# An attention and expert kernel on one Trainium2 core: the leftover keys' value product in four 64x64 tiles, and the order of the passes around it

## The chip, the cores and the metric

The kernel runs on one core of one Trainium2 chip. Its engines are named as the profile names them: PE (TensorE: matrix products, and transposes as products with the identity), DVE (VectorE), ACT (ScalarE), POOL (GpSimd) and SP (the queue that issues most DMAs). PE reads SBUF and writes PSUM, which has 8 banks of 2 KB in each of 128 partitions; DVE and ACT read PSUM and write SBUF.

The metric is the device time of one execution in microseconds (us). The kernel before was run three times: 1012.91, 1013.5 and 1015.62 us, a median of 1013.5.

## What is computed

Two stages. Eight batches of attention with 8 heads, 576 positions and head size 64, in which all probabilities below a threshold near the row's maximum are dropped; then its output, as 4608 rows of 512, goes through a router that gives each of 8 experts its 576 best rows, and through the experts.

```python
def _attn_ref(q, k, v, tau):
    scale = 1.0 / np.sqrt(q.shape[-1])
    scores = scale * np.matmul(q, k.transpose(0, 1, 3, 2))
    thresh = np.max(scores, axis=-1, keepdims=True) - tau
    scores = np.where(scores >= thresh, scores, -1000000000.0)
    scores = scores - np.max(scores, axis=-1, keepdims=True)
    attn = np.exp(scores)
    attn = attn / (np.sum(attn, axis=-1, keepdims=True) + 1e-09)
    return np.matmul(attn, v)
...
    for e in range(E):
        mask = assigned == e
        h = np.maximum(x[mask] @ w1[e], 0.0)
        out[mask] = h @ w2[e]
```

All products are in float32 in attention; the experts' use pairs of a rounded and a remainder part.

## The kernel before, in words

**Pairs, tiles, slots.** Attention takes two heads of a batch at a time: a pair `p`, four pairs a batch, 32 in all. A pair's scores are made in 9 tiles of 128 query rows by 576 keys (`score`, L70): tiles 0 to 7 alternate between the two heads, four each, and tile 8 holds the last 64 queries of both heads. Each tile `sc` has two PSUM banks, and the 576 keys stand as 288 columns in each; its two products use the two row halves of PE at once (64 rows by 128 columns), and tile 8 uses four tiles of 64x64 at once. A slot is two score tiles. The loop runs over 144 slots `s_`, and every engine works through its instructions in the order in which the loop emits them; each waits for what the others must have done first.

**What happens to a tile.** DVE scales it and takes its minimum (`mx`, L75, `z<-sc`), ACT takes the exponential (`ex`, L86), a slot later DVE drops what is below the threshold and sums (`stt`, L90), and one slot on PE transposes 512 of the 576 keys into the tile `tb` (`tr`, L99), two score tiles to one `tb`, of which there is one buffer of two banks. In the slot after that ACT copies them out to `pt` (`trev`, L114, L116).

**The leftover keys.** 64 keys of each row are left over: keys 512 to 575 of the first head and 0 to 63 of the second. Their transposes (`left`) go into the free columns behind the 288 of both `sc` buffers of one slot, the left slot: three of them into the first, two into the second. ACT copies them to `pl` (`leftev`, L125 to L127): the first head's keys to partitions 0 to 63, the second head's to 64 to 127. DVE's two passes `mx` of that slot are emitted behind all of these copies.

**The value product.** It is made transposed, in two halves `f` of 288 queries. A unit (`pv_unit`, L144) is two products of 128 keys by 64 columns, one for each head, side by side in the two column halves of one bank `xo`. Four units make one half, and `pl_unit` (L149) adds the leftovers to it, again as two products over all 128 partitions, with a `vt` that is zero where the other head's keys stand. So a pair has 8 units and 2 leftover units. When a half is done, ACT copies it to `xt` (L151).

**What sets the order.** A queue holds the units in order; at each slot's end `columns` takes from it as long as a credit lasts, which grows by 2.4 a slot up to 3.3, and as the unit's input is there (`when`). The first four units wait for tile 5's transposes, the others for tile 8's, the leftovers for `pl`. `xo` has two buffers, taken in turn by the halves and by `whole`, which fits in the batch's head work when no half is open: the sums' reciprocals (`rd_unit`, L165), the router's logits (`lg_unit`, L176, twice), their transposes (`lgt_unit`, L183, `lgm_unit`, L193) and, in the first two batches, five transposes of output rows (`xt_unit`, L205); those of the other batches come after the loop. `pt` has two buffers: before the first tile of pair p+2 is copied to it, the products of pair p must be done, and where they aren't, they are emitted in front of this copy (the `while` in the loop).

The diff touches `pv_unit`, `pl_unit`, `leftev`, `push_pair`, `columns`, `whole` and the loop.

Of the kernel before, what the change touches and what calls it, by code (L numbers as in the profile page):

```python
# [9 lines left out]
F32 = mybir.dt.float32  # L10
# [3 lines left out]
AF = mybir.ActivationFunctionType  # L14
# [8 lines left out]
def attention(ctx, tc, qk, vl, tau, wgd, xrows, xts, Lg, nb_batches, ident, swap, R, after_first):  # L23
    nc=tc.nc
# [6 lines left out]
    ps_t=ctx.enter_context(tc.tile_pool(name="ps_t",bufs=1,space=PSUM))  # L31
    ps_v=ctx.enter_context(tc.tile_pool(name="ps_v",bufs=2,space=PSUM))
    taub=cst.tile([128,1],F32,name="taub")
# [3 lines left out]
    LD={}  # L37
# [47 lines left out]
    def ex(t):  # L85
        A.activation(pview(t),ZB[t].rearrange("p a b -> p (a b)"),AF.Exp,bias=NBI[t][:,0:1],scale=-1.0)  # L86
# [8 lines left out]

    PT={}; PL={}; TB={}
    def turn(o,x):
# [12 lines left out]
    def trev(t):  # L110
        p,i=divmod(t,9); tb=TB.pop(t)
        if i==0: PT[p]=wk.tile([128,2,4,S],F32,name="pt"); PL[p]=wk.tile([128,S],F32,name="pl")
        if i<8:
            A.activation(PT[p][:,i%2,:,(i//2)*128:(i//2+1)*128].rearrange("p k (r q) -> p r k q",r=2),tb,AF.Copy)  # L114
        else:
            A.activation(PT[p][:,:,:,512:576],tb,AF.Copy)  # L116
    LB={}
    def left(p,n,t):
# [3 lines left out]
        if n: turn(sc[:,:,HS+64:HS+128],PB[p*9+8][:,512:640])  # L122
    def leftev(p):
        a=LB.pop((p,0)); b=LB.pop((p,1))
        A.activation(PL[p][:,0:384].rearrange("p (g r q) -> p r g q",g=3,r=2),a[:,:,HS:HS+192].rearrange("p r (g q) -> p r g q",g=3),AF.Copy)  # L125
        A.activation(PL[p][:,384:512].rearrange("p (r q) -> p r q",r=2),b[:,:,HS:HS+64],AF.Copy)
        for r in range(2): A.activation(PL[p][64*r:64*r+64,512:576],b[64*r:64*r+64,r,HS+64:HS+128],AF.Copy)  # L127

# [3 lines left out]

    banks=[]; VB={}
    def bank_v(sh):
        t=ps_v.tile(sh,F32,name="xo"); banks.append([False]); VB[id(t)]=banks[-1]
        return t
    def free_v(): return len(banks)<2 or banks[-2][0]
    def pv_unit(p,f,u):
        b,j=divmod(p,4)
        if b not in XT: XT[b]=wk.tile([128,4,S],F32,name="xt",bufs=XTB)  # L140
        if u==0: XO[p,f]=bank_v([128,512])
        xo=XO[p,f]; q=slice(f*HS,(f+1)*HS); v=LD[p]["v"]
        for h in range(2):
            T.matmul(xo[64*h:64*h+64,:HS],v[:,u,64*h:64*h+64],PT[p][:,h,u,q],start=(u==0),stop=False,skip_group_check=True)  # L144
    def pl_unit(p,f):
        b,j=divmod(p,4)
        q=slice(f*HS,(f+1)*HS); xo=XO.pop((p,f))
        for h in range(2):
            T.matmul(xo[64*h:64*h+64,:HS],LD[p]["v"][:,4,64*h:64*h+64],PL[p][:,q],start=False,stop=True,skip_group_check=True)  # L149
        if f==1: have[p,"pv"]=1  # L150
        return VB[id(xo)],lambda: A.activation(XT[b][:,j,q],xo[:,:HS],AF.Copy)  # L151
    def bank_g(b,sh):
        if b<nb_batches-1: return bank_v(sh)
# [47 lines left out]
    def xt_unit(b,c):  # L201
        ps=bank_v([128,4,128])
        n=128 if c<4 else 64
# [20 lines left out]
    def push_pair(p):  # L224
        b,j=divmod(p,4)
        def when(n): return lambda: have.get((p,n),1<<30)+HOLD<=st["slot"]
        if p==NP-1:


            def left(f):  # L230
                k,g=pl_unit(p,f); g(); k[0]=True
            for f in range(2):
                for u in range(4): queue.append(("c",when("t5" if f==0 else "t8"),u==0,lambda f=f,u=u: pv_unit(p,f,u)))
                if f==0: queue.append(("n",when("t8"),False,lambda: rd_calc(b)))
            for g in (lambda: rd_unit(b)(),lambda: left(0),lambda: left(1),lambda: lg_unit(b,0)(),lambda: lg_unit(b,1)(),lambda: lgt_unit(b)(),lambda: lgm_unit(b)()):
                queue.append(("n",when("pl"),False,g))
            queue.append(("n",lambda: not later,False,lambda: late.extend([lambda c=c: xt_unit(b,c) for c in range(5)])))
            return
        for f in range(2):
            for u in range(4): queue.append(("c",when("t5" if f==0 else "t8"),u==0,lambda f=f,u=u: pv_unit(p,f,u)))  # L240
            if (f,j)==(0,3): queue.append(("n",when("t8"),False,lambda: rd_calc(b)))
            queue.append(("c",when("pl"),False,lambda f=f: pl_unit(p,f)))
        if (b,j)==(0,0): queue.append(("n",lambda: True,False,R.consts))
        if (b,j)==(nb_batches-1,2): queue.append(("n",lambda: not aux,False,lambda: (R.prep(0,28),R.compare(R.k("E1"),J,0,28))))
        if j==3: queue.append(("n",lambda: not later,False,lambda: finish(b)))
    def finish(b):
# [6 lines left out]
    def flush():  # L253
        for k,g in later: g(); k[0]=True
        later.clear()
    def columns():
        while queue and queue[0][1]():
            if queue[0][0]=="c":
                if st["credit"]<1 or (queue[0][2] and not free_v()): return
                st["credit"]-=1  # L260
            c,_,_,g=queue.pop(0); r=g()
            if c=="c" and r:
                later.append(r)
                if aux: return
# [10 lines left out]
    after_first()  # L275
    ps=ps_v.tile([128,512],F32,name="xo")
# [93 lines left out]
class Router:  # L370
# [193 lines left out]
    def close(s): s.close1(); s.close2()  # L564
# [383 lines left out]
```

## Time and profile before

| What | us |
|---|---|
| median of three runs | 1013.5 |
| profiled execution, run time | 1010.9 |
| its span, first to last instruction | 1009.1 |
| attention's slots, about | 15 to 475 |
| router and experts | behind that |

The granted TensorE clock was 1.0 all through attention. A timeline row has the start in us from the span's start, the length in us from the first to the last of the merged instructions, engine, line, operation, out<-in, tile shape (for PE rows by columns of the array), operand shape and count; in square brackets the idle time before it and what ended it. A float32 product shows as two instructions, so that a value unit is x4 and a score tile is x4 (x8 where tile 8). PE instructions overlap in the array: what a step takes is read from its start to the start of the next.

### The profile page before, as it was taken

The page shows a single profiled execution, that of the slowest core. Times are in us where ns is not written, and L with a number is a line of the kernel's source. Part 1 is how long each engine was busy: PE and PEld are TensorE (multiplying, and loading weights), DVE is VectorE, ACT ScalarE, POOL GpSimd, SP SyncE. Part 2 cuts the span into 40 slices and gives each one's busy share as a digit, 9 for nine tenths or more (in the row PEclk, how much of TensorE's full clock was granted, in tenths as well). Part 3 has the DMA queues.
Part 4 walks back from the last instruction along what each step waited for, and adds up shares of the span by engine and source line. Part 5 has one row for each costly group of instructions (what it writes and reads, how often), then busy time and mean ns, then how long its engine had stood idle before and what let it go on. Part 6 is the DMA issues. An engine that isn't in the chain of part 4 may idle for free.

```text
span 1009.1 us, 24058 instructions
## 1 busy us (share of the span) xinstructions
PE 973.7 (96%) x9141; PEld 715.7 (71%) x9141; DVE 782.2 (78%) x2154; ACT 636.1 (63%) x1257; POOL 269.3 (27%) x443
## 2 busy tenths in 40 slices
PE   7999999999999999999879999999999999999996
PEld 4555555655655555555669789797887979899894
DVE  7999999999999999999578888788687787525220
ACT  6888888888888888888644344254342534545340
POOL 3333433333433343332020221212221203220202
PEclk9999999999999999999978999999999999999998
DMA  6322143243432133110771433434343415341101
GB/s 230 108 79 88 56 152 118 87 155 125 157 109 104 61 109 109 61 51 27 267 238 67 140 128 107 148 100 145 120 133 120 148 62 171 110 152 54 41 11 42
DMA packets 36004, 113.33 MB, mean 112 GB/s; under 512 B 4400, under 2 KB 5168, under 8 KB 35376
## 3 DMA queue, kind: packets, MB, share of 16 engines
q1 hardware_dynamic: 28496, 89.18, 25.1%
q0 software_dynamic: 5888, 19.03, 6.0%
q10 hardware_dynamic: 1504, 3.59, 1.1%
q8 instruction: 72, 1.18, 0.5%
q14 instruction: 44, 0.36, 0.1%
HBM read 89.34 MB, written 21.38 MB: 110 GB/s over the span
## 4 chain that ended last, share of the span: by engine, by line
PE 58%; DVE 19%; ACT 10%; issue 9%; DMA 2%; DVEq 0%; POOLq 0%; ACTq 0%
PE pf L781 21%; PE pf L813 19%; DVE z L75 7%; DVE pp L90 7%; ACT pp L86 5%; PE xo L144 5%; PE sc L70 4%; PE tb L99 3%; ACT pt L114 2%; PE pt L726 2%; ACT pt L116 1%; PE xo L205 1%; PE rps L434 1%; PE xo L149 1%; ACT pl L125 1%
## 5 line engine op out<-in xcount | busy, mean ns | idle before, releaser
L75 DVE TENSOR_SCALAR_CACHE_REDUCE z<-sc 128x576 f32<-128x576 f32 x288 | 205.8, 750 | 32.7 <-ACT pl L125 24.7
L76 POOL TENSOR_SCALAR nb<-nb,taub 128x1 f32<-128x1 f32 x288 | 146.5, 509 | 289.5 <-DVE z L75 255.9
L86 ACT ACTIVATE pp<-z,nb 128x576 f32<-128x576 f32 x256 | 187.7, 774 | 53.2 <-DVE z L75 52.5
L90 DVE SCALAR_TENSOR_TENSOR pp<-z,nb,pp 128x576 f32<-128x576 f32 x256 | 199.9, 812 | 0.3
L813 PE MATMUL pf<-w2h,H 128*128 128x512 f32 x576 | 195.1, 402 | 0.7 <-DVE H L366 0.7
L70 PE MATMUL sc<-qk 64*128 64x288 f32 (+1 forms) x1280 | 189.0, 432 | 2.6 <-DVE z L75 2.3
L144 PE MATMUL xo<-pt,vt 128*64 128x288 f32 x1024 | 151.7, 418 | 6.1 <-ACT xt L151 4.7
L114 ACT ACTIVATE pt<-tb 128x512 f32<-128x512 f32 x256 | 139.4, 591 | 8.8 <-PE tb L99 7.3
L813 PE MATMUL pf<-w2l,H 128*128 128x512 f32 x320 | 128.3, 401 | 0.0
L820 POOL DMA_INDIRECT out_dram<-y,idx x40 | 43.5, 1087 | 308.5 <-ACT y L816 248.9
L813 PEld LDWEIGHTS pf<-w2h,H 128*128 128x128 f32 x576 | 106.5, 189 | 20.0 <-DVE H L366 1.6
L70 PEld LDWEIGHTS sc<-qk 64*128 64x128 f32 (+1 forms) x1280 | 92.2, 180 | 30.2 <-DVE z L75 12.3
L144 PEld LDWEIGHTS xo<-pt,vt 128*64 128x64 f32 x1024 | 62.7, 136 | 70.3 <-issue 28.1
L99 PEld LDWEIGHTS tb<-ident,pp 64*128 64x128 f32 x2048 | 75.6, 139 | 50.9 <-issue 23.3
L781 PE MATMUL pf<-xh,w1h 128*128 128x288 f32 (+2 forms) x512 | 111.0, 303 | 0.7 <-ACT xh L727 0.7
L781 PE MATMUL pf<-xh,w1l 128*128 128x288 f32 (+2 forms) x512 | 110.6, 302 | 0.0
L781 PE MATMUL pf<-xl,w1h 128*128 128x288 f32 (+2 forms) x512 | 110.6, 302 | 0.0
L816 ACT ACTIVATE y<-pf 128x512 f32<-128x512 f32 x40 | 23.9, 598 | 127.0 <-PE pf L813 123.6
L99 PE MATMUL tb<-ident,pp 64*128 64x64 f32 x2048 | 94.3, 229 | 3.4 <-ACT pt L114 3.1
L793 ACT ACTIVATE hf<-pf 128x576 f32<-128x576 f32 x56 | 36.5, 653 | 89.5 <-PE pf L781 84.9
L781 PEld LDWEIGHTS pf<-xh,w1h 128*128 128x128 f32 x512 | 82.8, 192 | 1.5 <-ACT xh L727 1.1
L781 PEld LDWEIGHTS pf<-xh,w1l 128*128 128x128 f32 x512 | 82.6, 191 | 0.2
(199 smaller groups left out, 1358.4 us busy)
## 6 DMA issues: line engine op xcount, KB each, us to landing
qk<-qk_dram SPq DMA_DIRECT2D x31, 1008.0 KB, 5.0
w2s<-w_dram SPq DMA_DIRECT2D x32, 512.0 KB, 4.7
w1s<-w_dram SPq DMA_DIRECT2D x28, 512.0 KB, 5.2
vt<-vl_dram SPq DMA_DIRECT2D x32, 320.0 KB, 5.4
xrows<-pp SPq DMA_DIRECT2D x24, 260.0 KB, 2.3
xts<-xt SPq DMA_DIRECT2D x2, 1152.0 KB, 5.3
pt<-xts SPq DMA_DIRECT2D x2, 1152.0 KB, 7.5
xrows<-xr SPq DMA_DIRECT2D x8, 260.0 KB, 2.3
```

The lines of the kernel that those rows point to most:

```text
L70: T.matmul(sc[o,f,:HS], kd["q",h][r,c], kd[k,h][r,:],start=True,stop=True)
L75: V.tensor_scalar(z,SC.pop(t)[:,:,:HS],-0.125,None,op0=ALU.mult,op1=ALU.min,accum_out=nb[:,0:1])
L76: G.tensor_scalar(nb[:,1:2],nb[:,0:1],taub[:,0:1],None,op0=ALU.add)
L86: A.activation(pview(t),ZB[t].rearrange("p a b -> p (a b)"),AF.Exp,bias=NBI[t][:,0:1],scale=-1.0)
L90: V.scalar_tensor_tensor(pv,ZB.pop(t).rearrange("p a b -> p (a b)"),NBI[t][:,1:2],pv,op0=ALU.is_le,op1=ALU.mult,accum_out=den_of(p)[:,p%4, ...
L99: g=slice(64*r,64*r+64); T.transpose(o[:,r],x[g],ident[g,g])
L114: A.activation(PT[p][:,i%2,:,(i//2)*128:(i//2+1)*128].rearrange("p k (r q) -> p r k q",r=2),tb,AF.Copy)
L144: T.matmul(xo[64*h:64*h+64,:HS],v[:,u,64*h:64*h+64],PT[p][:,h,u,q],start=(u==0),stop=False,skip_group_check=True)
L781: T.matmul(ps[:,h,:n],s[w][:,k,f*128:(f+1)*128],s[x][:,k,cols[h]],start=(i==0),stop=(i==11))
L793: A.activation(hf,ps[:,:,:HS],AF.Relu)
L813: T.matmul(ps[:,0,:],H[:,f,c:c+128],s[w][:,f],start=(f==0 and j==0),stop=e)
L820: G.indirect_dma_start(out=out,out_offset=IOA(ap=s["idx"][:n,t:t+1],axis=0),in_=y[:n],in_offset=None)
```

## The change

**Leftovers.** `vt` now holds the leftover keys' values of both heads in both row halves, and two DMAs from SP move half of `pl` to the other partitions, into a new tile `px` (L132). `quad` (L165) makes the whole leftover product of a pair as four products of 64 keys by 64 columns: row half `f` of the array works on query half `f`, column half on the head, and the two row halves write two different `xo` banks. It is now the first of its pair: it opens both halves, and all eight units follow it. It is held until two slots after the left slot, and until both banks are free. The left slot itself is one slot earlier for even pairs.

**Banks.** The two `xo` banks are now fixed, one for each half. Head work uses the first bank whenever it is free, at most one piece a slot.

**Passes.** In every slot, DVE's first pass and the exponential are emitted, then the first leftovers' copy, then the second pass and exponential, then the second copies. A pair of score tiles that begins with tile 8 is swapped, so that the 64x64 score comes second.

```diff
-        if i==0: PT[p]=wk.tile([128,2,4,S],F32,name="pt"); PL[p]=wk.tile([128,S],F32,name="pl")
+        if i==0: PT[p]=wk.tile([128,2,4,S],F32,name="pt")
...
+    def leftev(p,n):
+        sc=LB.pop((p,n))
+        if n==0:
+            if p not in PL: PL[p]=wk.tile([128,S],F32,name="pl")
+            A.activation(PL[p][:,0:384].rearrange("p (g r q) -> p r g q",g=3,r=2),sc[:,:,HS:HS+192].rearrange("p r (g q) -> p r g q",g=3),AF.Copy)
+            return
+        A.activation(PL[p][:,384:512].rearrange("p (r q) -> p r q",r=2),sc[:,:,HS:HS+64],AF.Copy)
+        for r in range(2): A.activation(PL[p][64*r:64*r+64,512:576],sc[64*r:64*r+64,r,HS+64:HS+128],AF.Copy)
+        PX[p]=wk.tile([128,HS],F32,name="px")
+        nc.sync.dma_start(PX[p][0:64],PL[p][64:128,0:HS]); nc.sync.dma_start(PX[p][64:128],PL[p][0:64,HS:S])
...
+        st=open_v(p,f); e=p<NP-1 and u==3
...
-    def pl_unit(p,f):
...
-            T.matmul(xo[64*h:64*h+64,:HS],LD[p]["v"][:,4,64*h:64*h+64],PL[p][:,q],start=False,stop=True,skip_group_check=True)
...
+    def quad(p):
+        st=[open_v(p,f) for f in range(2)][0]; v=LD[p]["v"]
+        for f in range(2):
+            r=slice(64*f,64*f+64)
+            for h in range(2):
+                x=PL[p][r,f*HS:(f+1)*HS] if h==f else PX[p][r]
+                T.matmul(XO[p,f][64*h:64*h+64,:HS],v[r,4,64*h:64*h+64],x,start=st,stop=p==NP-1,skip_group_check=True)
...
+        due=when("pl")
+        queue.append(("c",lambda: due() and free[0] and free[1] and st["slot"]>=(9*p+13)//2,lambda: quad(p)))
+        queue.extend(units(0)+([calc] if j==3 else [])+units(1))
...
     def whole():
-        n=0
-        while n<2 and aux and not XO and free_v() and st["slot"]>=st["last"]+aux[0][0]:
-            r=aux.pop(0)[1](); n+=1; st["last"]=st["slot"]
-            later.append((banks[-1],r))
+        if aux and free[0] and st["slot"]>=st["last"]+aux[0][0]:
+            r=aux.pop(0)[1](); st["last"]=st["slot"]
+            def ev(): r(); free[0]=True
+            later.append(ev)
...
-        p8=[t//9 for t in ev_ if t%9==8]
+        if sc_ and sc_[0]%9==8: sc_.reverse()
+        p8=[p for p in range(NP) if (9*p+9)//2==s_]
...
-            p,i=divmod(t,9)
-            if i==5: push_pair(p)
-            if i==8: leftev(p); have[p,"pl"]=s_
-        for t in sc_:
-            mx(t)
-            ex(t)
+            if t%9==5: push_pair(t//9)
+        for n in range(2):
+            for t in sc_[n:n+1]: mx(t); ex(t)
+            for p in p8: leftev(p,n); have[p,"pl"]=s_
...
-        o[:,j,0:64,4,0:64]=v[:,2*j,512:576]; o[:,j,64:128,4,64:128]=v[:,2*j+1,0:64]
+        o[:,j,:,4]=np.tile(np.concatenate((v[:,2*j,512:576],v[:,2*j+1,0:64]),-1),(1,2,1))
```

Where the instructions stand. The first place is PE around the left slot of an odd pair, in a half batch without head work: `sc<-ident` are the leftovers' transposes, `tb` a slot's transposes, and the names in brackets are the engines waited for. Before:

```order
L99 MATMUL sc<-ident,pm 128x64 x2
L144 MATMUL xo<-pt,vt 64x288 x6
L99 MATMUL tb<-ident,pp 128x64 x16
L70 MATMUL sc<-qk 128x288 x4
L144 MATMUL xo<-pt,vt 64x288 x2
L149 MATMUL xo<-pl,vt 64x288 x2
L99 MATMUL tb<-ident,pp 128x64 x16
```

And now, with the waits, from the same transposes on:

```order
L99 MATMUL sc<-ident,pm 128x64 [waits Pool_49]
L99 MATMUL sc<-ident,pm 128x64
L151 MATMUL xo<-pt,vt 64x288 x2
L99 MATMUL tb<-ident,pp 128x64 [waits DVE_49,PE_49,Activation_49]
L99 MATMUL tb<-ident,pp 128x64 x7
L99 MATMUL tb<-ident,pp 128x64 [waits DVE_49]
L99 MATMUL tb<-ident,pp 128x64 x7
L70 MATMUL sc<-qk 128x288 [waits DVE_49,Activation_49]
L70 MATMUL sc<-qk 128x288
L70 MATMUL sc<-qk 128x288 [waits DVE_49,Activation_49]
L70 MATMUL sc<-qk 128x288
L99 MATMUL tb<-ident,pp 128x64 [waits DVE_49,PE_49,Activation_49]
```

Three units in the left slot have become one, and the unit and the leftovers of the next slot are gone from it; both score tiles of that slot now wait for ACT too: the first for the first copy to `pl`, the second for the last one.

The second place is ACT around the left slot of an even pair. Before:

```order
L116 ACTIVATE pt<-tb 128x8x64
L114 ACTIVATE pt<-tb 128x2x4x64
L125 ACTIVATE pl<-sc 128x2x3x64
L126 ACTIVATE pl<-sc 128x128
L127 ACTIVATE pl<-sc 64x64 x2
L86 ACTIVATE pp<-z,nb 128x576 x2
L114 ACTIVATE pt<-tb 128x2x4x64 x2
```

Now:

```order
L86 ACTIVATE pp<-z,nb 128x576
L127 ACTIVATE pl<-sc 128x2x3x64
L86 ACTIVATE pp<-z,nb 128x576
L129 ACTIVATE pl<-sc 128x128
L130 ACTIVATE pl<-sc 64x64 x2
L116 ACTIVATE pt<-tb 128x8x64
L157 ACTIVATE xt<-xo 128x288
L114 ACTIVATE pt<-tb 128x2x4x64
L86 ACTIVATE pp<-z,nb 128x576 x2
```

The copies to `pl` stand behind the exponentials of their slot instead of in front of them, and a copy of a finished half (`xt`) now stands between the copy of tile 8 and that of the next pair's first tile.

The third place is PE at the same even pair, from its left slot to the quad, now:

```order
L99 MATMUL sc<-ident,pm 128x64 x2
L151 MATMUL xo<-pt,vt 64x288 x6
L207 MATMUL xo<-ident,lt 128x128
L99 MATMUL tb<-ident,pm 128x64 x8
L99 MATMUL tb<-ident,pp 128x64 x8
L70 MATMUL sc<-qk 128x288 x4
L151 MATMUL xo<-pt,vt 64x288 x2
L99 MATMUL tb<-ident,pp 128x64 x16
L70 MATMUL sc<-qk 128x288 x2
L70 MATMUL sc<-qk 64x288 x4
L165 MATMUL xo<-pl,vt 64x288
L165 MATMUL xo<-px,vt 64x288 x2
```

The last unit of the pair before stands alone behind the next slot's scores, and it is this unit that the `xt` copy above belongs to. The quad follows the 64x64 score.

More of the change, by code (lines that the diff above doesn't have):

```diff
@@ L31, in attention @@
     ps_t=ctx.enter_context(tc.tile_pool(name="ps_t",bufs=1,space=PSUM))
-    ps_v=ctx.enter_context(tc.tile_pool(name="ps_v",bufs=2,space=PSUM))
+    ps_v=[ctx.enter_context(tc.tile_pool(name="ps_v%d"%f,bufs=1,space=PSUM)) for f in range(2)]
     taub=cst.tile([128,1],F32,name="taub")
@@ L122, in left, with bank_v, open_v @@
         if n: turn(sc[:,:,HS+64:HS+128],PB[p*9+8][:,512:640])
[L123 to L127, printed above, removed]
+    def leftev(p,n):
[8 more added lines that the diff above has]
+        nc.sync.dma_start(PX[p][0:64],PL[p][64:128,0:HS]); nc.sync.dma_start(PX[p][64:128],PL[p][0:64,HS:S])
     have={}
     XT={}; XO={}
[L133 to L137, printed above, removed]
+    free=[True,True]
+    def bank_v(f,sh=(128,512)):
+        free[f]=False
+        return ps_v[f].tile(list(sh),F32,name="xo")
+    def open_v(p,f):
+        if (p,f) not in XO: XO[p,f]=bank_v(f); return True
+        return False
     def pv_unit(p,f,u):
@@ L226, in when, with units @@
         def when(n): return lambda: have.get((p,n),1<<30)+HOLD<=st["slot"]
+        def units(f): return [("c",lambda w=when("t5" if f==0 else "t8"),u=u: w() and (u>0 or (p,f) in XO or free[f]),lambda u=u: pv_unit(p,f,u)) for u in range(4)]
+        calc=("n",when("t8"),lambda: rd_calc(b))
         if p==NP-1:
[L230 to L234, printed above, removed]
@@ L243, in push_pair, with left @@
-        if (b,j)==(0,0): queue.append(("n",lambda: True,False,R.consts))
-        if (b,j)==(nb_batches-1,2): queue.append(("n",lambda: not aux,False,lambda: (R.prep(0,28),R.compare(R.k("E1"),J,0,28))))
-        if j==3: queue.append(("n",lambda: not later,False,lambda: finish(b)))
+            def left():
+                quad(p)
+                for f in range(2): close(p,f)()
+            queue.extend(units(0)+[calc]+units(1))
+            for g in (lambda: rd_unit(b)(),left,lambda: lg_unit(b,0)(),lambda: lg_unit(b,1)(),lambda: lgt_unit(b)(),lambda: lgm_unit(b)()):
+                queue.append(("n",when("pl"),g))
@@ new lines, in push_pair @@
+            queue.append(("n",lambda: not later,lambda: late.extend([lambda c=c: xt_unit(b,c) for c in range(5)])))
+            return
+        due=when("pl")
+        queue.append(("c",lambda: due() and free[0] and free[1] and st["slot"]>=(9*p+13)//2,lambda: quad(p)))
+        queue.extend(units(0)+([calc] if j==3 else [])+units(1))
+        if (b,j)==(0,0): queue.append(("n",lambda: True,R.consts))
+        if (b,j)==(nb_batches-1,2): queue.append(("n",lambda: not aux,lambda: (R.prep(0,28),R.compare(R.k("E1"),J,0,28))))
@@ L246, in finish @@
+        if j==3: queue.append(("n",lambda: not later,lambda: finish(b)))
     def finish(b):
@@ L253, in flush @@
     def flush():
-        for k,g in later: g(); k[0]=True
+        for g in later: g()
         later.clear()
@@ L275, in attention @@
     after_first()
-    ps=ps_v.tile([128,512],F32,name="xo")
+    ps=ps_v[0].tile([128,512],F32,name="xo")
     def idles(n):
```

36 lines of the change are left out of this document (14 added, 22 removed).

## The prediction

> **What bounds the kernel now.** I read the page's busy line first, then attention's stretch by itself, then its waits.
>
> ```profile
> PE 973.7 (96%) x9141; PEld 715.7 (71%) x9141; DVE 782.2 (78%) x2154; ACT 636.1 (63%) x1257; POOL 269.3 (27%) x443
> ```
> ```profile
> 15.00:475.00 460.00, 449.70 (x5249) 264.05 (x5251) 431.39 (x1236) 397.75 (x763) 165.99 (x333) 1.00 0.28 98
> ```
> ```profile
> L75 DVE TENSOR_SCALAR_CACHE_REDUCE z<-sc 128x576 f32<-128x576 f32 x282 | 201.3, 750 | 27.1 <-ACT pl L125 24.7 <-PE sc L70 1.8
> ...
> PE xo L144 <- ACT xt L151: 4.7, 12, 1.2
> PE tb L99 <- ACT pt L114: 3.1, 6, 1.0
> ```
> The change touches attention alone. There (15 to 475 us) PE is busy 449.7 of 460 us, VectorE 431.4, ScalarE 397.8: TensorE sets the pace, VectorE is 4% behind it. The stretch holds 282 of 288 score tiles, so a batch of 36 tiles (18 slots of two) takes 460/282x36 = 58.7 us. PE's listed waits are 4.7+3.1 = 7.8 us, 1.0 per batch. VectorE's 24.7 us behind L125, the wait which the moved pass removes, is idle time of an engine that isn't the bound: its removal is worth between nothing and all of the 24.7 to PE; I take nothing, as beside a bound engine, and the layout below contains the moved pass anyway.
>
> One left slot shows the step lengths (start, length, engine): PE, then ScalarE, then VectorE.
>
> ```profile
> 318.79 0.70 PE L70 MATMUL sc<-qk 64*128 64x288 f32 x4
> 319.33 0.35 PE L99 MATMUL sc<-ident,pp 64*128 64x64 f32 x6
> 319.51 0.70 PE L70 MATMUL sc<-qk 64*128 64x288 f32 x4
> 320.05 0.22 PE L99 MATMUL sc<-ident,pp 64*128 64x64 f32 x2
> 320.11 0.23 PE L99 MATMUL sc<-ident,pm 64*128 64x64 f32 x2
> 320.26 1.19 PE L144 MATMUL xo<-pt,vt 128*64 128x288 f32 x8
> 321.38 0.71 PE L99 MATMUL tb<-ident,pp 64*128 64x64 f32 x16
> 321.93 1.35 PE L70 MATMUL sc<-qk 64*128 64x288 f32 x12
> 323.21 0.71 PE L149 MATMUL xo<-pl,vt 128*64 128x288 f32 x4
> 323.85 0.39 PE L165 MATMUL xo<-rd,swap 128*128 128x4 f32 x2
> ...
> 329.71 0.71 PE L144 MATMUL xo<-pt,vt 128*64 128x288 f32 x4
> 330.25 0.66 PE L149 MATMUL xo<-pl,vt 128*64 128x288 f32 x4
> 330.83 0.69 PE L176 MATMUL xo<-xt,wg 128*32 128x288 f32 x8
> 331.45 0.46 PE L99 MATMUL tb<-ident,pp 64*128 64x64 f32 x8
> ```
> ```profile
> 318.10 1.45 ACT L86 ACTIVATE pp<-z,nb 128x576 f32<-128x576 f32 x2
> 319.46 0.58 ACT L116 ACTIVATE pt<-tb 128x512 f32<-128x512 f32 x1
> 319.94 0.59 ACT L114 ACTIVATE pt<-tb 128x512 f32<-128x512 f32 x1
> 320.41 0.49 ACT L125 ACTIVATE pl<-sc 128x384 f32<-128x384 f32 x1
> 320.78 0.29 ACT L126 ACTIVATE pl<-sc 128x128 f32<-128x128 f32 x1
> 320.94 0.45 ACT L127 ACTIVATE pl<-sc 64x64 f32<-64x64 f32 x2
> 321.74 1.45 ACT L86 ACTIVATE pp<-z,nb 128x576 f32<-128x576 f32 x2 [0.35 <-DVE z L75]
> ...
> 325.99 0.39 ACT L151 ACTIVATE xt<-xo 128x288 f32<-128x288 f32 x1
> 326.28 1.07 ACT L114 ACTIVATE pt<-tb 128x512 f32<-128x512 f32 x2
> ```
> ```profile
> 320.94 0.76 DVE L75 TENSOR_SCALAR_CACHE_REDUCE z<-sc 128x576 f32<-128x576 f32 x1 [0.72 <-ACT pl L125]
> ```
> From start to next start: a score tile 0.54 us, the first leftovers' transposes 0.18, the second 0.21, a value unit 0.54 (329.71 to 330.25), a slot's transposes 0.55; a change of tile shape adds 0.05 to 0.10 (the 0.54 unit takes 0.58 or 0.64 in front of another shape). ScalarE: exp 0.68, a transposed pair's eviction 0.48 to the next and 0.59 long, the leftovers' evictions 0.37, 0.16 and 0.45, XT 0.29. Exp starts 0.80 after the pass that feeds it (320.94, 321.74).
>
> **What the change removes.** A pair's leftovers are now two units of two column halves, 2x0.54. Four 64x64 tiles at once take one unit if all run together. The score of tile 8 has that shape: x12 at 321.93 is one tile (0.54) and this quad, which with two changes of shape ends at 323.21, so 1.28-0.54 = 0.74 less up to 0.2 is 0.54 to 0.64. I take 0.54; the other end is two passes (rival C). The new quad stands right behind a 64x64 score, and the even pairs' scores swap places for it: about 0.1 less in changes. So 0.54+0.1 per pair, **2.5 us per batch**. The old waits of L144 and L99, 1.0 per batch, should go too: banks are asked for later.
>
> **What it adds.** Two DMAs per pair on SP, a move of 64 rows of 1152 B (72 KB each) between partitions.
>
> ```profile
> z<-y ACTq DMA_DIRECT2D x8, 128.0 KB, 2.3
> qk<-qk_dram SPq DMA_DIRECT2D x31, 1008.0 KB, 5.0
> ```
> The like move takes 2.3 us to landing; bounds are 2.0 and, behind a load on its queue, 5.0. It can be issued when the last pl eviction ends, 4.1 us into an odd pair's left slot (below), so with about 0.5 for its issue it lands at 6.9. PE, free again at 5.43 (below), has a slot's transposes (0.55), a score (0.64 with its change), the 64x64 score (0.54) and the quad's first half (0.27) ahead of the matmul that reads px: 7.4. So it is hidden by 0.5 us; landing 1 us later would cost PE 0.5 in each of 16 odd pairs, 8 us. SP's next load stands behind it, some 20 us ahead of its use: nothing.
>
> **What it moves.** Two new waits, both seen in the order, both on PE, hence on the path. I lay the slot out from the first score's start (0), using the steps above; the first pass starts when the first transposes are done, by
>
> ```profile
> 167.98 1.19 PE L70 MATMUL sc<-qk 64*128 64x288 f32 x8
> 168.74 0.76 DVE L75 TENSOR_SCALAR_CACHE_REDUCE z<-sc 128x576 f32<-128x576 f32 x1 [0.37 <-PE sc L70]
> ...
> 458.89 0.71 PE L99 MATMUL tb<-ident,pp 64*128 64x64 f32 x16
> 459.44 1.19 PE L70 MATMUL sc<-qk 64*128 64x288 f32 x8
> 459.64 1.08 ACT L114 ACTIVATE pt<-tb 128x512 f32<-128x512 f32 x2
> ```
> 0.22 us behind the run's 0.54, and ScalarE follows transposes by 0.20 behind their 0.55.
>
> *Odd pairs.* PE: 0 score, 0.54 transposes, 0.72 score, 1.26 transposes, 1.47 one unit, 2.05 slot's transposes, 2.60 free. VectorE's pass at 0.94. ScalarE: exp 1.74, first eviction 2.42 to 2.92, exp 2.79, then 3.47 and 3.63 to 4.08. The next slot's scores write the same two buffers: the first waits for 2.92, the second for 4.08 (4.15 with the signal), so they end at 4.69 where free running gives 3.68. That slot holds no value unit (they were used up, since the quad put all of them after it), so its transposes come at once and need tb: XT 4.0, evictions 4.29 and 4.77 to 5.36, PE at 5.43. PE loses 1.0+0.75 = **1.75 us**. In the half of a batch in which head work stands there (a logit unit of 0.62 in the first slot, 330.83 to 331.45, its transpose, by the row transposes below some 0.6, in the second), the same steps give 0.39+0.44 = **0.83**.
>
> *Even pairs.* Three units in the left slot: free at 3.67, scores to 4.79, and then the pair's last unit, which the eviction of the next pair's first tile waits for: unit done 5.6, XT to 5.9, eviction to 6.5, PE's transposes at 6.55 instead of 5.38. **1.2 us**, or 0.9 where the small rd product stands there.
>
> In both, behind the waiting transposes stand the next scores, and VectorE waits for these: by the same steps its pass one slot later finds no score for 0.3 to 0.6 us, so PE's loss isn't caught up.
>
> A batch has two of each: 0.83+1.75+1.2+0.9 = 4.7. **Sum per batch: 58.7-2.5-1.0+4.7 = 59.9, +1.2.** The first batch starts without head work or an earlier pair, and I leave it at its old time; seven batches give +8.4. Besides, the first two batches' rows are transposed as head work, ten units:
>
> ```profile
> 205.34 0.66 PE L205 MATMUL xo<-ident,xt 128*128 128x128 f32 x4
> 205.98 0.71 PE L99 MATMUL tb<-ident,pp 64*128 64x64 f32 x16
> ```
> 0.64 each from start to next start. About a third of them stand where PE now waits: -2.2. Together +6.2: a span of 1015.3 for 1009.1, a run of 1017.1 for the profiled 1010.9. That run lies 2.6 below the median, so **1019.5** on its scale. The last pair's quad, behind attention, I leave out (under 1 us).
>
> The Trainium skill (TensorEngine Tiling (Array Packing), "PSUM Bottleneck") says that tiling speeds up TensorE but not the emptying of PSUM, which may become the limit. By totals it doesn't bind here (ScalarE is busy 397.8 of 460 us), and by totals alone the sum would keep the whole gain; by its order, as laid out above, it does.
>
> **Rivals.**
> A, *not slower*: PE comes late to the odd pairs' second score. If it gets there 1.6 us later than laid out (more head work, a later unit), ScalarE is ahead and the 0.83 and 1.75 vanish: 1.2-2.6 = -1.4 per batch, x7 = -10, less 1 that the rows no longer hide: 1004.5. With the even pairs' wait gone too, 995. For it: PE was the late engine everywhere before. Against it: ScalarE's chain hangs on PE's own first score, so lateness before the slot moves both.
> B, *no change*: the head work and rows fill the gaps wholly. Without filler they are 2x(1.75+1.2) = 5.9 per batch; if all 2.4 of head work lies inside, 3.5 is left, just what is saved (2.5+1.0): 1013.5. Against it: two of its five pieces stand in slots that are full.
> C, *the quad isn't one pass*: 31 x 0.54 = 17 on top: 1036. Late DMAs end nearby. The Trainium skill (same page, "Gotcha 1: PSUM Pressure") says that different row tiles can't write one PSUM bank at once; here each row half has its own bank, which by that rule leaves one pass.
>
> **How the numbers follow.** Forecast 0.55 (its own range 1013 to 1026: the steps are good to 0.3 per half batch, 5 us in all), A 0.22, B 0.15, C 0.08. A measurement here can tell 0.3%, 3 us. Slower: three quarters of the forecast, C, a little of B: 0.51. Same: a fifth of the forecast, most of B: 0.24. Faster: A and the rest: 0.25. Range 1003 to 1029: it takes in A's own time and leaves C and A's far end out.
>
> **What would show it.** L75's wait behind pl gone; PE's score L70 waiting for the pl evictions once per pair and its tb transposes for pt or xt, some 35 us in all against 7.8; quads about 0.54 us from the next unit; no PE wait on px. Wrong, if PE shows these waits under 20 us: then it is A. If VectorE waits little for scores, PE isn't the bound and the sum is off.

## The result, and the profile after

The changed kernel took 1050.1 us in the median of four runs (1048.0 to 1056.8), the kernel before 1014.6: a ratio of 1.036 (1.031 to 1.041). The prediction had 1019.5, with a range that ended at 1029. The direction was right; the loss is six times the one foretold. The profiled execution took 1050.3 us, with a span of 1048.5 against 1009.1, so 39.4 us are to be found (the medians differ by 35.5).

First the busy line of the changed kernel's page, and attention's stretch by itself (length, then busy time of PE, PEld, DVE, ACT and POOL, granted clock, DMA share, GB/s).

```profile
PE 977.4 (93%) x9141; PEld 715.2 (68%) x9141; DVE 786.1 (75%) x2154; ACT 636.2 (61%) x1257; POOL 266.9 (25%) x443
```
```profile
15.00:480.00 465.00, 435.81 (x5203) 252.89 (x5207) 431.90 (x1226) 393.69 (x759) 162.56 (x331) 1.00 0.32 107
```

Up to the first pass of the last score tile PE is now busy for 435.8 us, where the kernel before has 447.2 (15 to 471.31 us). So the four tiles at once do save work; but the stretch is no shorter. How far each kernel has come at the end of attention is read from the first pass of the last score tile (start, length, engine), in the kernel before and then in the changed one.

```profile
471.31 0.75 DVE L75 TENSOR_SCALAR_CACHE_REDUCE z<-sc 128x576 f32<-128x576 f32 x1
```
```profile
480.05 0.75 DVE L75 TENSOR_SCALAR_CACHE_REDUCE z<-sc 128x576 f32<-128x576 f32 x1
```

Attention is 8.7 us later. That is near the 6.2 that was forecast, and leaves 30 us that lie elsewhere. Behind attention stand the 30 row transposes of six batches (L205 before, L219 after), with router steps between them. PE's timeline, of the kernel before and of the changed one, shows the first rows and the first router product behind the last row (`rps<-gq`).

```profile
485.47 1.04 PE L205 MATMUL xo<-ident,xt 128*128 128x128 f32 x8
486.75 2.59 PE L205 MATMUL xo<-ident,xt 128*128 128x128 f32 x16 [0.25 <-ACT pp L215]
...
511.25 0.21 PE L512 MATMUL rps<-gq,trib 128*128 128x72 bf16 x1 [1.17 <-DVE gq L366]
```
```profile
494.81 0.60 PE L219 MATMUL xo<-ident,xt 128*128 128x128 f32 x4
496.10 0.66 PE L219 MATMUL xo<-ident,xt 128*128 128x128 f32 x4 [0.69 <-ACT pp L229]
497.45 0.66 PE L219 MATMUL xo<-ident,xt 128*128 128x128 f32 x4 [0.69 <-ACT pp L229]
...
502.30 1.11 PE L219 MATMUL xo<-ident,xt 128*128 128x128 f32 x4 [0.68 <-ACT pp L229]
...
547.80 0.24 PE L523 MATMUL rps<-gq,trib 128*128 128x72 bf16 x1 [0.35 <-DVE gq L377]
```

Before, the transposes of several rows follow one another (x16 is four rows). Now each row stands alone (x4), behind 0.69 us of waiting for ScalarE's copy of the row before. The stage takes 547.80-494.81 = 53.0 us instead of 511.25-485.47 = 25.8: 27.2 us more. The likely cause is a line of the diff in `xt_unit`, `ps=bank_v(0,[128,4,128])`; the list of what the diff touches, ahead of the prediction, lacks this function. The rows used to take the two `xo` banks in turn, and now they always take the first. ScalarE's rows of the changed kernel show the other half of the cycle.

```profile
495.45 0.60 ACT L229 ACTIVATE pp<-xo 128x512 f32<-128x512 f32 x1 [1.19 <-PE xo L219]
...
496.80 0.60 ACT L229 ACTIVATE pp<-xo 128x512 f32<-128x512 f32 x1 [0.65 <-PE xo L219]
```

0.60 for the transposes, 0.60 for the copy and the hand-overs make 1.35 us a row; neither engine works while the other does. After three rows a second thing sets in: the same four transposes take 1.11 instead of 0.66. The windows of the two kernels show the clock beside it (before, then after; it is the third number from the end).

```profile
500.00:512.00 12.00, 8.50 (x101) 6.52 (x99) 7.21 (x22) 8.11 (x26) 0.00 (x0) 1.00 0.77 277
```
```profile
495.00:501.00 6.00, 3.25 (x19) 2.07 (x18) 2.81 (x11) 2.78 (x8) 0.00 (x0) 0.82 0.58 231
501.00:510.00 9.00, 5.93 (x36) 4.45 (x35) 1.88 (x8) 3.47 (x10) 0.00 (x0) 0.50 0.39 135
```

With PE busy for 3.25 of 6.00 us the granted clock fell, and it stayed at 0.50 to the end of the stage. Before, with 8.50 of 12.00 us, it stayed at 1.00.

The whole difference, by the starts quoted above: attention 8.7, from the last pass to the first row 0.6 (14.76 against 14.16), the rows 27.2, router and experts behind them 2.9 (1048.5-547.80 against 1009.1-511.25). That makes 39.4.

### The profile page after: what moved, and what is told of

Its sections match the earlier page's. It is cut to its first block, busy times and chain, and to the rows that moved or that the text cites. A ratio compares the mean times of both kernels' runs of the same rounds, so it can differ in the third digit from the quotient of the medians.

```text
span 1048.5 us, 24286 instructions
## 1 busy us (share of the span) xinstructions
PE 977.4 (93%) x9141; PEld 715.2 (68%) x9141; DVE 786.1 (75%) x2154; ACT 636.2 (61%) x1257; POOL 266.9 (25%) x443
## 4 chain that ended last, share of the span: by engine, by line
PE 75%; ACT 9%; DVE 7%; issue 7%; DMA 2%; POOLq 0%; DVEq 0%; SPq 0%; POOL 0%; ACTq 0%
PE pf L792 20%; PE pf L824 17%; PE xo L151 11%; PE sc L70 10%; PE tb L99 7%; ACT pt L114 2%; PE xo L165 2%; ACT pp L229 2%; PE pt L737 2%; DVE pp L90 1%; DVE z L75 1%; PE xo L219 1%; ACT xt L157 1%; ACT pp L86 1%; PE rps L445 1%
## 5 line engine op out<-in xcount | busy, mean ns | idle before, releaser
L76 POOL TENSOR_SCALAR nb<-nb,taub 128x1 f32<-128x1 f32 x288 | 142.6, 495 | 290.8 <-DVE z L75 226.9
L86 ACT ACTIVATE pp<-z,nb 128x576 f32<-128x576 f32 x256 | 190.5, 776 | 38.9 <-DVE z L75 34.8
L70 PE MATMUL sc<-qk 64*128 64x288 f32 (+1 forms) x1280 | 193.6, 435 | 8.4 <-ACT pl L130 3.1
L114 ACT ACTIVATE pt<-tb 128x512 f32<-128x512 f32 x256 | 140.0, 597 | 24.8 <-PE tb L99 24.8
```

The lines of the kernel that those rows point to most:

```text
L70: T.matmul(sc[o,f,:HS], kd["q",h][r,c], kd[k,h][r,:],start=True,stop=True)
L76: G.tensor_scalar(nb[:,1:2],nb[:,0:1],taub[:,0:1],None,op0=ALU.add)
```

## Experiments on the rows behind attention

All ratios are against the kernel before, run on the same chip, with their 95% interval. Its own median was between 1009.4 and 1014.6 us on the chips used, so that differences of ratios are the fair comparison; 0.001 is 1 us.

**Two banks for the rows.** The changed kernel, with this edit alone:

```diff
+    nl=[0]
     def xt_unit(b,c):
-        ps=bank_v(0,[128,4,128])
+        if b>=nb_batches-NDEF-NBO: nl[0]+=1
+        ps=bank_v(nl[0]%2,[128,4,128])
```

> The changed kernel with one thing undone: the 30 row transposes behind attention take the two xo banks in turn again, as before the change; attention is untouched. Theory (one bank): the loss behind attention is that each row transpose must wait for ScalarE's copy of the one before out of the only bank, 52.7 us for 30 rows (494.8 to 547.5) against 24.6 before (485.5 to 510.1). Then about 27 us go: 1023 us (1019 to 1026), and the clock stays at 1.00 there. Rival (late inputs or a low clock that has another cause): the rows stay as slow whatever the bank, 1045 us or more. By the first forecast's attention terms alone (+6.2) it would be 1020.

1021.7 us, ratio 1.0083 (1.0062 to 1.0104). PE's timeline and a window of this run:

```profile
495.11 1.04 PE L221 MATMUL xo<-ident,xt 128*128 128x128 f32 x8
496.40 2.59 PE L221 MATMUL xo<-ident,xt 128*128 128x128 f32 x16 [0.25 <-ACT pp L231]
...
520.89 0.21 PE L525 MATMUL rps<-gq,trib 128*128 128x72 bf16 x1 [1.17 <-DVE gq L379]
```
```profile
501.00:510.00 9.00, 7.14 (x86) 5.80 (x86) 5.82 (x21) 6.74 (x22) 0.00 (x0) 1.00 0.87 300
```

The stage is back at 25.8 us and the clock at 1.00. About 28 of the 36 us came from this one line.

**One bank in the kernel before.** The reverse: the 30 rows of the kernel before share one bank, and nothing else is changed.

```diff
+    one=[]
     def xt_unit(b,c):
-        ps=bank_v([128,4,128])
+        if b<nb_batches-NDEF-NBO: ps=bank_v([128,4,128])
+        else:
+            if not one: one.append(ps_v.tile([128,4,128],F32,name="xo"))
+            ps=one[0]
```

> The kernel before, with the one edit that its 30 row transposes behind attention all go into one xo bank. Theory (one bank): the same loss as in the changed kernel, without any of its attention: 27 us on top, 1041 us (1038 to 1044), and the granted clock falls to 0.5 in that stretch. Rival (the loss belongs to something else of the change, such as later inputs): no more than 1018.

1042.1 us, ratio 1.0283 (1.0260 to 1.0307). A window shows the same state of the clock:

```profile
501.00:510.00 9.00, 6.27 (x39) 4.96 (x39) 2.80 (x15) 3.27 (x11) 0.00 (x0) 0.50 0.36 126
```

So the loss needs nothing of the new attention: the single bank alone makes it, in either kernel.

**The gaps filled.** The changed kernel with its one bank; behind each row's transposes PE gets eleven small products of zeros into the other bank.

```diff
+    ps=ps_v[1].tile([128,512],F32,name="xo")
...
-            now=at; late.pop(0)()(); at=now+XTY
+            now=at; g=late.pop(0)(); idles(11); g(); at=now+XTY
```

> The changed kernel as it is, with eleven small bfloat16 products of zeros into the other xo bank behind each of the 30 rows' transposes, so that PE is busy while it waits for ScalarE. It tells the wait's own share from the clock's. Theory (the wait opens gaps, the gaps bring the clock to 0.5, and that doubles the transposes, too): at clock 1.00 a row takes 0.6 for the transposes and 0.7 for ScalarE, 1.3 as the first three rows did, so 30 x 1.33 = 40 us in place of 52.7: 1038 us (1034 to 1041). Rival (the clock costs nothing because ScalarE's round trip sets the pace, and the products only delay): 1050 or more.

1038.1 us, ratio 1.0241 (1.0217 to 1.0264): 12 us less, by nothing but useless work. PE's timeline, and a window:

```profile
494.57 0.66 PE L219 MATMUL xo<-ident,xt 128*128 128x128 f32 x4
495.06 0.78 PE L290 MATMUL xo<-idle 128*128 128x128 bf16 x11
495.91 0.66 PE L219 MATMUL xo<-ident,xt 128*128 128x128 f32 x4
```
```profile
501.00:510.00 9.00, 8.43 (x125) 7.79 (x123) 3.60 (x16) 4.47 (x14) 0.00 (x0) 1.00 0.53 181
```

A row takes 1.34 us, and the clock stayed at 1.00 to the end of the stage, which is 42.6 us long. Of the 28 us, then, 16 are the alternation of two engines on one bank and 12 are the clock, which fell where PE had its gaps. The Trainium skill (TensorE: Matmul & The Clock Gate, "Part 1: The HAM clock gate") says that the array runs at half clock unless recent activity releases it, and in "HAM oscillation" that idle gaps beyond about 3.4 us bring the half clock back. The half agrees with the 0.50 here. The 3.4 us don't: gaps of 0.7 us each were enough, since filling them kept the clock up. The section "A second HAM failure mode: psum-queue depth-cycling" tells of such short gaps between groups. What the limit is, these runs don't show. It isn't the length of a single gap: in the kernel before, PE waited 0.76 us at 494.8 and 0.81 at 500.8 in one piece and kept 1.00. Nor is it a plain busy share: the run with the quad between the halves, below, has PE busy for 3.16 of 6.00 us from 512 to 518, 53%, and kept 1.00 there.

## Experiments on attention

The rest of the loss, 0.8%, is nearly all in attention. PE's waits there in the changed kernel (total, times, longest):

```profile
PE tb L99 <- ACT pt L114: 21.2, 32, 1.0
PE sc L70 <- ACT pl L130: 3.1, 8, 0.4
...
PE sc L70 <- ACT pl L127: 0.8, 1, 0.8
```

The timeline shows both predicted places: PE around an odd pair's left slot, and around an even pair's.

```profile
311.53 0.71 PE L151 MATMUL xo<-pt,vt 128*64 128x288 f32 x4
312.16 0.72 PE L99 MATMUL tb<-ident,pp 64*128 64x64 f32 x16
312.99 0.76 PE L70 MATMUL sc<-qk 64*128 64x288 f32 x4
314.16 0.76 PE L70 MATMUL sc<-qk 64*128 64x288 f32 x4 [0.42 <-ACT pl L130]
315.57 0.72 PE L99 MATMUL tb<-ident,pp 64*128 64x64 f32 x16 [0.66 <-ACT pt L114]
...
325.98 1.58 PE L70 MATMUL sc<-qk 64*128 64x288 f32 x8
327.50 0.71 PE L151 MATMUL xo<-pt,vt 128*64 128x288 f32 x4
328.13 0.39 PE L179 MATMUL xo<-rd,swap 128*128 128x4 f32 x2
329.20 0.71 PE L99 MATMUL tb<-ident,pp 64*128 64x64 f32 x16 [0.68 <-ACT pt L114]
329.75 1.35 PE L70 MATMUL sc<-qk 64*128 64x288 f32 x12
330.92 0.40 PE L165 MATMUL xo<-pl,vt 64*64 64x288 f32 x1
...
331.52 1.19 PE L151 MATMUL xo<-pt,vt 128*64 128x288 f32 x8
```

From start to next start, the odd pair's transposes take 0.83 instead of 0.55, its first score 1.17 instead of 0.54, and then come 0.66 of listed wait: 0.28+0.63+0.66 = 1.57 us. Only 1.08 of it stand in brackets; starvation that merely stretches a run of instructions is seen by comparing pitches. (With a pitch for the last step too, 1.41 instead of 0.54, it is 0.87 and the sum 1.78.) In the even pair two scores take 1.52 instead of 1.12, and 0.68 are waited: 1.08. The quad takes 331.52-330.92 = 0.60.

**The quads of odd pairs uncounted.** Two banks for the rows as above, and:

```diff
-        queue.append(("c",lambda: due() and free[0] and free[1] and st["slot"]>=(9*p+13)//2,lambda: quad(p)))
+        queue.append(("n" if p%2 else "c",lambda: due() and free[0] and free[1] and st["slot"]>=(9*p+13)//2,lambda: quad(p)))
```

> As the run with two banks for the rows, and the quads of odd pairs take nothing of the credit, so that three units follow them instead of two and the pair's last unit stands in the next left slot, not alone behind the next scores with the xt copy in front of tile 8's successor. Theory (the even pairs' wait is from that forced unit): PE's waits of 1.0 and 0.68 us for the eviction behind the xt copy go or fall under 0.4; the unit itself (0.58) only moves; about 0.6 per even pair, 16 pairs: 9 us less than the run with two banks, 1014 us (1011 to 1017). Rival (ScalarE's own backlog sets that wait): within 3 us of that run.

1019.7 us, ratio 1.0054 (1.0032 to 1.0075), 0.003 below the run with two banks, and the intervals overlap: a miss. PE's waits in attention in this run:

```profile
PE tb L99 <- ACT pt L114: 10.4, 20, 1.0
PE xo L165 <- PE sc L70: 3.7, 5, 0.7
...
PE xo L165 <- DVE xr L229: 2.6, 4, 0.9
PE xo L165 <- DVE rm L183: 2.2, 2, 1.1
```

The forced unit was indeed what half of the `pt` waits came from (21.1 to 10.4), but 7.5 of the 10.7 us came back as waits in front of the quad (8.5 instead of 1.0). The quad opens both banks, so whatever moved earlier into them, it waits for. At the first pass of the last score tile this run's profile is 3.2 us ahead of the run with two banks (477.14 against 480.35), but 2.6 of these lie in the first batch, where the granted clock stayed at 1.00; in the other run, as in the changed kernel, it was 0.50 from 28 to 31 us. The later batches together gained 0.3.

**The pl copies ahead again.** Two banks for the rows, and the passes in their old order:

```diff
         for n in range(2):
-            for t in sc_[n:n+1]: mx(t); ex(t)
             for p in p8: leftev(p,n); have[p,"pl"]=s_
+        for t in sc_: mx(t); ex(t)
```

> The run with two banks for the rows (1021.7), with the pl copies emitted ahead of both passes and exponentials again, as before the change; the quad stays as it is. Theory (ScalarE's order makes the wait: pl copies behind the exponentials): PE's score products no longer wait for pl, about 1.4 us per batch in the trace, VectorE's wait behind the first copy (24.7 us before) comes back and costs PE nothing: 11 us less, 1011 us (1007 to 1015). Rival (it is ScalarE's backlog in that slot, whatever its order: the exponentials and with them the next copies just come later): within 4 us of 1021.7.

1026.8 us, ratio 1.0171 (1.0154 to 1.0187): 9 us more, where the theory had 11 less. VectorE's and PE's waits in attention:

```profile
DVE z L75 <- ACT pl L127: 36.1, 30, 2.2
```
```profile
PE tb L99 <- ACT pt L114: 24.8, 30, 1.5
PE xo L197 <- ACT lt L192: 4.1, 7, 0.6
```

PE's waits for `pl`, 4.2 us, are gone from its list. But VectorE's passes stand behind the copies again, 1.2 us a time, and two groups of PE's waits grew: those for `pt` from 21.1 to 24.8 us, and those in front of the quad and of head work (`lt` is its largest) from 1.0 to 11.1. The second to fourth batch, in which output rows are transposed as head work, are 1.0, 2.6 and 1.7 us longer, the others 0.2 to 0.4. Both theories are wrong: the order does matter, in the opposite sense. That VectorE's wait delays the exponentials, and these ScalarE's later copies, fits the lists, but no run tests it.

**The old product in the quad's place.** Two banks for the rows; four products over all 128 partitions, the zero-padded values, no moves to `px`:

```diff
...
-            r=slice(64*f,64*f+64)
             for h in range(2):
-                x=PL[p][r,f*HS:(f+1)*HS] if h==f else PX[p][r]
-                T.matmul(XO[p,f][64*h:64*h+64,:HS],v[r,4,64*h:64*h+64],x,start=st,stop=p==NP-1,skip_group_check=True)
+                T.matmul(XO[p,f][64*h:64*h+64,:HS],v[:,4,64*h:64*h+64],PL[p][:,f*HS:(f+1)*HS],start=st,stop=p==NP-1,skip_group_check=True)
...
```

> The run with two banks for the rows (1021.7), with the quad replaced at its own place by the old product, two for each half over all 128 partitions with the zero-padded values, and without the two moves to px. It measures what the four 64x64 tiles at once are worth in the new order. Theory (PE sets the pace between the waits): 0.54 per pair and the changes of shape, 2.0 per batch, 16 us more: 1038 us (1034 to 1041). Rival (PE has idle time enough there, and the product is hidden): 1021 to 1028. PE waits on px would show as a gain instead.

1030.3 us, ratio 1.0198 (1.0183 to 1.0213). Against 1.0083 the four tiles are worth 11.5 us: neither the 16 of the theory nor a hidden product. A later batch took 61.09 us instead of 59.37 from first pass to first pass, 1.7 more.

**The quad between the halves.** It ends the first half and opens the second, so that the first four units needn't wait for it:

```diff
-        st=open_v(p,f); e=p<NP-1 and u==3
+        st=open_v(p,f); e=p<NP-1 and (f,u)==(1,3)
...
-            r=slice(64*f,64*f+64)
+            st=open_v(p,f); r=slice(64*f,64*f+64)
...
+        if p<NP-1: return close(p,0)
...
-        queue.append(("c",lambda: due() and free[0] and free[1] and st["slot"]>=(9*p+13)//2,lambda: quad(p)))
-        queue.extend(units(0)+([calc] if j==3 else [])+units(1))
+        queue.extend(units(0)+([calc] if j==3 else [])+[("c",lambda: due() and free[1] and st["slot"]>=(9*p+13)//2,lambda: quad(p))]+units(1))
```

> The run with two banks for the rows (1021.7), with the quad put between the two halves of its pair: it ends the first half and opens the second. The first half's four units no longer wait for it and fill the slots in which PE had none. Theory (the odd pairs' waits come from slots left empty of units): PE's waits for pl and for tb in odd pairs, together 2.3 per batch, go, the even pairs' 0.8 stays: 18 us less, 1003 us (999 to 1008). Rival (ScalarE sets the pace there, and the units only take the place of waits while other slots are emptied): within 5 us of 1021.7.

1010.2 us, ratio 1.0003 (0.9992 to 1.0013): 8 us less than with the quad first, under half of what was expected. PE's waits for `pt` fell from 21.1 to 4.3 us; new waits of 7.6 in all came up behind the copies of head work, most of them in front of a half's first unit, which needs the bank that head work has. Inside the loop, though, nearly all of the expected 18 us came: the first pass of the last score tile starts at 464.35, 16.0 us earlier than with two banks for the rows (480.35). From there to the first row it takes 23.0 us instead of 14.8, so 8.3 are lost again. PE's timeline shows what stands there:

```profile
470.33 0.69 PE L191 MATMUL xo<-xt,wg 128*32 128x288 f32 x8
472.58 1.19 PE L191 MATMUL xo<-xt,wg 128*32 128x288 f32 x8 [1.56 <-ACT lt L193]
474.30 1.11 PE L198 MATMUL xo<-ident,lt 128*128 128x128 f32 x4 [0.53 <-ACT lt L193]
476.08 0.45 PE L208 MATMUL xo<-ident,lt 128*128 128x128 f32 x1 [0.67 <-DVE lw L203]
476.84 6.92 PE L151 MATMUL xo<-pt,vt 128*64 128x288 f32 x32 [0.31 <-DVE lwm L213]
...
487.39 1.04 PE L222 MATMUL xo<-ident,xt 128*128 128x128 f32 x8
```

It is the head work of the last batch but one, which with the quad first was done by 475 us, inside the loop. Here head work falls behind, and at the end each piece waits for the copy of the one before out of the first bank (that it finds this bank free too seldom is borne out by the run with either bank, below). The clock falls with it (0.52 from 472 to 481 us), so that eight units take 6.92 us instead of the 4.10 of the kernel before.

**The same, with the pl copies ahead.** On top of that, the edit that put the pl copies ahead of the passes, as shown above:

> The run before this one (quad between the halves), with the pl copies ahead of the passes and exponentials, as before the change. It asks what the new order of the passes is worth once PE has work there. If PE comes late, neither order holds it: within 4 us of that run. If the new order is what frees VectorE and the exponentials, 8 us or more above it.

1004.3 us, ratio 0.9947 (0.9931 to 0.9963): the best of all, faster than both kernels. Here the old order gains 5.6 us where with the quad first it cost 9; in the profiles 4.6 us lie in the loop and 2.3 behind it, where the head work is as late but the clock is 0.92 on average instead of 0.78. VectorE's waits and attention's stretch in this run:

```profile
DVE z L75 <- ACT pl L127: 17.4, 22, 1.4
```
```profile
15.00:465.00 450.00, 431.47 (x5264) 258.55 (x5266) 429.02 (x1232) 398.20 (x765) 162.53 (x333) 1.00 0.32 110
```

Both engines are now busy for 95 to 96% of the stretch. That PE has units to work on while VectorE waits fits this, but is not tested by itself.

**Head work in either bank.** On top of that, head work may use the second bank, too.

```diff
-        if b<nb_batches-1: return bank_v(0,sh)
+        if b<nb_batches-1: return bank_v(hb[0],sh)
...
-        if aux and free[0] and st["slot"]>=st["last"]+aux[0][0]:
+        hb[0]=f=1 if free[1] else 0
+        if aux and free[f] and st["slot"]>=st["last"]+aux[0][0]:
...
```

> The run with the quad between the halves and the pl copies ahead (ratio 0.9947), with head work allowed into the second xo bank too, which it takes whenever that one is free. In that run PE waits some 8 us in all for ScalarE's and VectorE's copies of head work out of the first bank, before the first unit of a half. Theory: these waits go, 6 us, ratio 0.989 (0.986 to 0.993). Rival (the waits move to the quad, which opens the second bank): 0.9947 within 0.002.

1006.9 us, ratio 0.9965 (0.9952 to 0.9978): the rival's number, but not its place. PE's waits behind head work nearly went, and its waits for `pt`, not those in front of the quad (1.6 us), rose: from 4.9 to 11.4 us. Behind the loop it is now 15.2 us to the first row instead of 20.7, so that the late head work is cured; but the loop is 9.7 us longer.

**The old product between the halves.** The run with ratio 0.9947, with the quad replaced by the old product over all partitions, as in the edit shown above:

> The run with the quad between the halves and the pl copies ahead (ratio 0.9947), with the quad replaced at its place by the old product over all 128 partitions and without the moves to px. It measures what the four tiles at once are worth where PE has few waits. In the order with the quad first they were worth 11.7 us. Theory (there a part of it only lengthened waits): the full 2.0 per batch here, 16 us, ratio 1.010 (1.008 to 1.013). Rival (the same 11.7 or less): 1.006 or less.

1014.0 us, ratio 1.0042 (1.0026 to 1.0057), 9.5 us above the quad. In two kernels, then, the quad is worth 10 to 12 us; more than that it doesn't save with PE better supplied either.

**The order of the passes alone, in the kernel before.**

```diff
...
-            if i==8: leftev(p); have[p,"pl"]=s_
-        for t in sc_:
-            mx(t)
-            ex(t)
+        for n in range(2):
+            for t in sc_[n:n+1]: mx(t); ex(t)
+            for p in p8: leftev(p,n); have[p,"pl"]=s_
```

> The kernel before with the change's new order of the passes alone: in the left slot the first pass and exponential, then the first pl copy, then the second pass and exponential, then the other copies. Nothing else is changed. Theory (PE is the late engine there; its next scores wait for the pl copies, which now stand behind the exponentials): as between the two runs with the quad between the halves, 6 us slower, ratio 1.006 (1.003 to 1.010), and VectorE's 24.7 us behind the first copy are gone without a gain. Rival (VectorE's wait held the whole): ratio 0.995 or less.

1011.9 us, ratio 1.0020 (1.0010 to 1.0030): 2 us slower, between the two. The first batch is 4.4 us longer (60.2 against 55.8 between first passes), with one wait of 2.0 us for the first `pl` copy, behind which the clock is 0.52 from 43 to 50 us (1.00 before); later batches are as long as before (58.4 and 58.0 against 58.4 and 58.5). So the loss is in the first batch alone.

## Why the prediction was wrong

- **"The change touches attention alone"** is the step that failed. The row transposes behind attention are made by `xt_unit`, which the change moves to one bank, as its diff shows; the prediction has no term for these 30 rows, and of the work behind attention it leaves out only the last pair's quad, as under 1 us. Two runs show its size from both sides: 28 us back by a second bank, 28 us lost by taking it from the kernel before. The trace of before would have given about half: the transposes (0.62 to 0.66 a row) and ScalarE's copy in turn, 1.35 a row as it came out, against 25.8/30 = 0.86, so 15 us. The other 12 are the falling clock, and the filled gaps told the two apart.
- **Attention's new waits** were right. Predicted per batch: 1.75 and 0.83 for odd pairs, 1.2 and 0.9 for even ones, 4.7 in all. Measured: 1.57 and, in the half batch with head work, 0.77 (1.56 instead of 1.12 for two scores, then 0.33), 1.00 and 1.08: 4.4 (4.8 with pitches throughout). Two later batches grew by 1.0 and 0.8 us, where 1.2 was forecast. PE's listed waits for `pt` and `pl` are 25.1 us, above the 20 below which rival A was to hold. Rival A (these waits vanish) and B (head work hides them) are out.
- **The quad's 2.5 per batch** was too much. It is one pass, 0.60 to the next unit, so rival C is out; but replacing it cost 1.7 per batch in one order and some 1.5 in the other (58.5 against 57.0).
- **The first batch "left at its old time"** was wrong: it grew by 3.0 us (58.8 against 55.8). Pairs 1 to 3 of it have an earlier pair, and at pair 0's left slot the units that used to be there now stand behind the quad. With the quad between the halves and the same passes it takes 57.0. Part of the 3.0 is the clock: behind PE's waits at 24 to 28 us, of up to 0.85 us, it fell in the changed kernel, where it was 1.00 before. That cost some 1.7 us if PE set the pace there (an estimate: from 27 to 32 us the clock is 0.66 on average, so a third of 5 us). What makes up the rest was not tried. A window of the changed kernel:

```profile
28.00:31.00 3.00, 3.00 (x26) 1.36 (x24) 2.54 (x7) 2.46 (x5) 1.07 (x2) 0.50 0.83 328
```

- **The 2.2 us for rows that fall into gaps** didn't come: batches two to five grew by 0.8 on average, like the later ones.
- **VectorE's wait priced at nothing**: nearly right for the kernel before, where the new order took it away and the time rose by 0.2%, all of it in the first batch. It isn't a property of the wait, though. With the quad first, the order that brings such a wait back costs 9 us.
- **The moves to px** were hidden, as forecast: 1.9 us to landing, and no PE wait behind them.

The sum for attention was 6.2 us against 8.7 measured; the chance of "slower" went to the right side, for a reason that covers a quarter of the loss. The other three quarters come from a term which the prediction didn't have; that the change came out as clearly slower as it did is luck. The 2.9 us in router and experts were not followed up: with two banks they were 1.1 (498.91 against 497.85), and with one bank and the gaps filled 2.7 (500.50), so the clock that the rows leave behind isn't the reason. Two slips of the sums change nothing: 1017.1 and 2.6 make 1019.7, not 1019.5, and rival A without both waits of the even pairs (1.2 and 0.9) would be near 990, not 995.

## What to carry to other kernels

When a change takes a buffer away from a pool, list every user of that pool in the whole program, and for each one ask what its cycle becomes when producer and consumer take turns: the sum of both, not the larger. A stage that leaves PE idle about half the time can pay twice, as this one did, when the clock falls with it. The same reordering can help or hurt, as the order of the passes did here, so it has to be tried again whenever the work around it moves. And a loop that got shorter may only have put work off: look at what stands behind it, too.

## What was not expected of the hardware

Gaps of 0.7 us each, with PE busy for 54% of 6 us, were enough to bring the granted clock to 0.50, and it stayed there for the rest of the stage, although PE, at the lower clock, was busy for 66% of the time (5.93 of 9.00 us). With 71% (8.50 of 12.00) at full clock it stayed at 1.00, and once with 53% of 6 us, so these shares are no rule. Products of zeros that do nothing made a kernel 12 us faster.
